# Attention pairs taken by twos, v loaded and weighed by pair, own x buffers for the first three batches

## The chip, the cores and the metric

The kernel runs on one core of a Trainium2 chip. The metric is device time in microseconds; the runs shown are whole executions without a profile, and one more execution was profiled. TensorE is called PE in the profile, VectorE DVE, ScalarE ACT, GpSimd POOL; SP is the engine whose queue issues most transfers.

## The reference

Two blocks follow each other. The first is a causal attention over 8 batches, 8 heads, 576 tokens and 64 numbers a head, whose scores get a bias from a running sum of `s`:

```
scores = q @ k.T / 8 + min(-(cum[i] - cum[j]), 0)     # cum = cumsum(max(s, 0)); later keys masked
x = softmax(scores) @ v                               # 8 batches x 576 tokens x 512
```

The second sends each token of `x` to one of 8 experts. The expert is the largest of 8 logits, unless a gate says that the token keeps the expert of the token before it; the output is the softmax weight of that expert times a two-layer network:

```
out[token] = p[e] * (relu(x @ w1[e]) @ w2[e])         # 512 -> 1024 -> 512
```

All numbers are float32.

## The kernel before

**Pairs.** The attention works on pairs of heads: 8 batches with 4 pairs each, 32 pairs in all (`NPAIR`). A pair's q and k lie in 128 partitions, one head in each half. Scores are computed with keys on the partitions. `scores(n, u)` does one of four units of pair n: matmuls (L869) into a PSUM buffer `ps` of which there are three, an exponential on ScalarE (L870) into a tile `e`, and the causal mask on GpSimd (L855). `values(n, j0, j1)` multiplies the `e` tiles with v (L894) for the token blocks 0 to 5 (PSUM tile `po0`) or 6 to 8 (`po6`), and its `evacuate` takes the reciprocal of the row sums (L900, kept in `recs`) and writes the scaled result into the batch's x tile `xb` (L901). `turn(n)` transposes the pair's part of x (L912) for the router's matmuls.

**Weighed v.** The bias is a product of two factors, so v is multiplied by a factor per key: `weigh` does this on VectorE (L841, for the first batch `weigh_heads`, L851) from the loaded tile `va` into the tiles `vg`, and `ones_column` copies the factor itself beside it on ScalarE (L833). v is loaded by batch, and there are two sets of `vg`, one for odd and one for even batches.

**Order.** The program order is written by hand and each engine keeps it. Slot n of the main loop issues the scores of pair n and then the values of pair n - 1:

```
for u in range(len(UNITS)):
    scores(n, u)
    if u == 1: at(n, 0)
values(n - 1, 0, NJA)()
at(n, 1)
values(n - 1, NJA, NJ)()
turn(n - 1)
at(n, 3)
```

Weighing and loads stand between these lines. `plan(slot, place, f)` notes work of the router, and `at(slot, place)` issues it there.

**Router.** The router works on groups of two batches (`GB`). For a group it runs `product` (matmuls into `lp`, L208) and `logits` (copies on VectorE, L217 to L226), `codes` (L233 to L245 on VectorE, with one exponential `ex` on ScalarE at L242), `turn1`, `turn2` (VectorE), `ranks` (matmuls into `pos`, L289 and L290, in one of the three buffers of the scores), `rows` and `gates` (VectorE), and then 18 scatters (`put`, L337 on GpSimd) that store the tokens of x in a table in the chip's main memory, sorted by expert. The fourth group's steps run in the experts' part.

**x tiles.** The pool `p_x` has four buffers; a small scratch for the key factors takes one, and the batches follow in turn.

**Experts.** `Experts.run` follows: units of up to 256 tokens, layer 1 (L568) and layer 2 (L592), with weights of one expert, 4 MB, loaded for each unit. The first unit's weights go into the pool `w_first` while the attention still runs; `fetch` reads its tokens from the table.

## Time and profile before

| | us |
|---|---|
| median of 3 runs (lowest, highest) | 740.49 (739.32, 741.26) |
| the profiled execution, its own time | 751.67 |
| its span, from the first to the last instruction | 749.9 |
| attention, up to the first expert matmul | 224.45 |
| TensorE busy in the span | 733.6 |
| ScalarE busy | 162.2 |
| VectorE busy | 246.8 |
| GpSimd busy | 209.4 |

A line of the groups names the line of the code, the engine, the operation, what is written from what, the shape and the count, then the busy time and the mean of one in ns, and after the second bar the time that the engine stood idle just before, with what ended it. A line of the timeline has the start in us, the duration in us, engine, line and operation, the count of merged instructions, and in brackets the idle time before it and what ended that. Matmul ends are modelled, so the starts are read. "issue" is time in which the engine waited for nothing that the profile shows.

### The profile page before, as it was taken

The page shows a single profiled execution, that of the slowest core. Times are in us where ns is not written, and L with a number is a line of the kernel's source. Part 1 is how long each engine was busy: PE and PEld are TensorE (multiplying, and loading weights), DVE is VectorE, ACT ScalarE, POOL GpSimd, SP SyncE. Part 2 cuts the span into 40 slices and gives each one's busy share as a digit, 9 for nine tenths or more (in the row PEclk, how much of TensorE's full clock was granted, in tenths as well). Part 3 has the DMA queues.
Part 4 walks back from the last instruction along what each step waited for, and adds up shares of the span by engine and source line. Part 5 has one row for each costly group of instructions (what it writes and reads, how often), then busy time and mean ns, then how long its engine had stood idle before and what let it go on. Part 6 is the DMA issues. An engine that isn't in the chain of part 4 may idle for free.

```text
span 749.9 us, 16025 instructions
## 1 busy us (share of the span) xinstructions
PE 733.6 (98%) x6509; PEld 501.5 (67%) x6509; DVE 246.8 (33%) x653; ACT 162.2 (22%) x318; POOL 209.4 (28%) x452
## 2 busy tenths in 40 slices
PE   8999999999999999999999999999999999999996
PEld 5888878877877667657657375537645676637674
DVE  4655756766765552101100511140142001050110
ACT  4554544443431011001001010101110111101110
POOL 2643376577575245330100101010101001000110
PEclk9999999999999999999999999999999999999999
DMA  6764464566679776698537969996999965999000
GB/s 205 249 198 130 146 203 140 189 197 200 214 224 369 243 301 212 257 409 227 219 131 224 377 195 397 365 393 241 423 324 370 413 215 227 297 394 339 30 15 32
DMA packets 55524, 186.23 MB, mean 248 GB/s; under 512 B 11661, under 2 KB 32525, under 8 KB 47120
## 3 DMA queue, kind: packets, MB, share of 16 engines
q1 hardware_dynamic: 48640, 165.01, 62.4%
q0 software_dynamic: 6800, 20.09, 7.1%
q8 instruction: 53, 0.87, 0.5%
q14 instruction: 31, 0.25, 0.1%
HBM read 164.46 MB, written 20.88 MB: 247 GB/s over the span
## 4 chain that ended last, share of the span: by engine, by line
PE 95%; issue 1%; DVE 1%; POOL 1%; ACT 0%; POOLq 0%; ACTq 0%
PE yp L592 34%; PE hp L568 31%; PE po L894 13%; PE ps L869 12%; PE hp L559 4%; PE lp L208 1%; POOL table L337 0%; ACT e L870 0%; PE pos L289 0%; POOL e L855 0%; PE pos L290 0%; DVE y L595 0%; POOL out_dram L597 0%; DVE xb L901 0%; POOLq L93 0%
## 5 line engine op out<-in xcount | busy, mean ns | idle before, releaser
L592 PE MATMUL yp<-w2b,hT 128*128 128x512 f32 (+2 forms) x752 | 259.3, 593 | 0.0
L568 PE MATMUL hp<-xT,w1b 128*128 128x256 f32 (+1 forms) x1216 | 233.2, 352 | 0.0
L568 PEld LDWEIGHTS hp<-xT,w1b 128*128 128x128 f32 x1216 | 206.2, 190 | 32.6 <-issue 7.5
L592 PEld LDWEIGHTS yp<-w2b,hT 128*128 128x128 f32 (+2 forms) x752 | 107.9, 167 | 141.0 <-issue 139.6
L597 POOL DMA_INDIRECT out_dram<-y,gi x37 | 36.5, 987 | 416.4 <-DVE y L595 391.5
L570 ACT ACTIVATE hT<-hp 128x256 f32<-128x256 f32 (+1 forms) x152 | 54.0, 355 | 430.7 <-PE hp L568 421.0
L595 DVE TENSOR_SCALAR y<-yp,gi 128x512 f32<-128x512 f32 x37 | 27.6, 746 | 304.6 <-PE yp L592 291.9
L870 ACT ACTIVATE e<-ps 128x768 f32<-128x768 f32 (+1 forms) x128 | 97.3, 837 | 104.3 <-PE ps L869 93.7
L894 PE MATMUL po<-vg,e 128*64 128x66 f32 x3200 | 106.7, 224 | 5.9 <-issue 3.6
L894 PEld LDWEIGHTS po<-vg,e 128*64 128x64 f32 x3200 | 99.2, 138 | 11.3 <-issue 7.2
L869 PE MATMUL ps<-qb,kb 64*128 64x192 f32 (+4 forms) x768 | 98.6, 402 | 0.8 <-ACT e L870 0.8
L869 PEld LDWEIGHTS ps<-qb,kb 64*128 64x128 f32 x768 | 67.3, 187 | 31.6 <-ACT e L870 9.5
L337 POOL DMA_INDIRECT table<-xb,idx x72 | 74.4, 1033 | 32.2 <-issue 23.0
L855 POOL TENSOR_SCALAR_AFFINE_SELECT e<-e 128x256 f32<-128x256 f32 (+1 forms) x160 | 64.0, 421 | 63.0 <-ACT e L870 62.2
L579 DVE STREAM_TRANSPOSE hT<-hs 32x256 f32<-32x256 f32 x64 | 27.9, 436 | 74.8 <-ACT hs L561 74.0
L900 DVE RECIPROCAL recs<-po 128x12 f32<-128x12 f32 x64 | 13.4, 209 | 63.1 <-PE po L894 55.7
L901 DVE TENSOR_TENSOR xb<-po,recs 128x384 f32<-128x384 f32 x64 | 29.3, 458 | 3.1 <-POOL xb L313 0.5
L841 DVE TENSOR_TENSOR vg<-va,wk 128x1024 f32<-128x1024 f32 (+1 forms) x21 | 29.4, 1400 | 2.2 <-DMA va<-in_vm_dram 2.2
L538 DVE STREAM_TRANSPOSE xT<-xq 128x1024 f32<-128x1024 f32 (+1 forms) x23 | 23.7, 1028 | 18.7 <-DMA xq<-table 18.5
L559 PE MATMUL hp<-w1b,xT 128*32 128x512 f32 (+1 forms) x224 | 28.3, 594 | 0.0
L912 DVE STREAM_TRANSPOSE xt<-xb 128x576 f32<-128x576 f32 x32 | 24.9, 778 | 2.9 <-PE lp L208 1.4
L559 PEld LDWEIGHTS hp<-w1b,xT 128*32 128x32 f32 (+1 forms) x224 | 8.1, 114 | 17.7 <-issue 17.6
(222 smaller groups left out, 165.7 us busy)
## 6 DMA issues: line engine op xcount, KB each, us to landing
w1b<-in_w_dram SPq DMA_DIRECT2D x29, 2048.0 KB
w2b<-in_w_dram SPq DMA_DIRECT2D x29, 2048.0 KB
kb<-in_k_dram SPq DMA_DIRECT2D x32, 288.0 KB
qb<-in_q_dram SPq DMA_DIRECT2D x32, 288.0 KB
xq<-table SPq DMA_DIRECT2D x56, 130.0 KB
va<-in_vm_dram SPq DMA_DIRECT2D x7, 1024.0 KB
w1b<-in_w_dram SPq DMA_DIRECT2D x4, 512.0 KB
w2b<-in_w_dram SPq DMA_DIRECT2D x4, 512.0 KB
```

Of the source, the lines that this page charges most:

```text
L337: put = self.nc.gpsimd.indirect_dma_start(out=self.halves, in_=src, element_offset=0, in_offset=None, out_offset=bass.IndirectOffsetOnAxis ...
L559: mm(ps[d, :], lhsT=xT[:, k, d], rhs=self.ws[l][0][:, k, c * 512 : c * 512 + 512], start=(k == 0), stop=(k == DK - 1))
L568: mm(ps[:, :w], lhsT=self.ws[ls[0]][0][:, k, c * P : c * P + P], rhs=xT[:, k, :w], start=(k == 0), stop=(k == DK - 1))
L570: nc.scalar.activation(self.hT[u][:, c, :w], ps[:, :w], Act.Relu)
L592: mm(ps[d, :], lhsT=hT[:, k, n * P + d.start : n * P + d.stop], rhs=self.ws[l][1][:, k, :], start=(k == 0), stop=(k == FK - 1))
L597: put = nc.gpsimd.indirect_dma_start(out=self.out[:, :], out_offset=bass.IndirectOffsetOnAxis(ap=gi.bitcast(I32)[:, n, 0:1], axis=0), in_= ...
L841: nc.vector.tensor_tensor(vgs[b % 2][g][:, c0:c1].rearrange("p c h e -> p (c h) e")[:, :, :DH], va[:, c0:c1].rearrange("p c h e -> p (c h) ...
L855: nc.gpsimd.affine_select(out=ap, in_=ap, compare_op=Alu.is_ge, fill=0.0, base=base, pattern=n, channel_multiplier=-1)
L869: mm(ps[:, h, at : at + z - a], lhsT=kb[d, key : key + P], rhs=qb[d, a:z], start=True, stop=True)
L870: nc.scalar.activation(e, ps, Act.Exp, scale=scale)
L894: mm(po[d, j - j0, :], lhsT=weights_of(n, c, j, h), rhs=vg[:, c, 2 * hp + h, :], start=(c == 0), stop=(c == last))
L901: nc.vector.tensor_tensor(xb[:, j0:j1, :, 32 * hp : 32 * hp + 32], po[:, :, :DH].rearrange("p j (g i) -> p j g i", g=2), rec[:, :, 0].unsq ...
```

## The change

The loop now runs over 16 slots m of two pairs, 2m and 2m + 1. A slot issues the scores of both pairs, then the values of both, then both turns, then the weighing for the two pairs that come two slots later. v comes from the host already laid out by pair, with zeros for the missing tokens of the last block; a pair is one load of 320 KB into one of four `va` buffers, and is weighed by two VectorE operations and one ScalarE copy into one of four `vg` tiles. The x tiles of batches 0 and 1 lie in the space of the first expert's weights (`w_first`), that of batch 2 in a tile of its own, and only the later ones in `p_x`. The router's steps move to places of the new slots: 0 and 1 after the scores of the first and second pair, 3 and 4 after their values, 5 at the end of the slot. Its constants are set in two parts.

```diff
-PARTS = ((0, 1), (1, HP))
+NV = 4
+STORES = (((4, 5), (0, 1, 3, 4, 5), (0, 1, 3, 4, 5), (0, 1, 3, 4, 5), (0,)), ((4, 5, 5), (0, 1, 3, 4, 5), (0, 1, 3, 4, 5), (0, 1, 3, 4, 5)),
+          ((4, 5), (0, 0, 1, 1, 3, 4, 5, 5)))
+BX = 3
...
-    def load_v(b):
-        if b >= B:
+    def load_v(n):
+        if n >= NPAIR:
             return
-        nc.sync.dma_start(va[:, :NF], vm[b])
-        nc.sync.dma_start(va[TL:, NF], vt[b])
+        b, hp = divmod(n, HP)
+        va = vs[n] = p_v.tile([P, NB, 2, DH], F32, name="va")
+        nc.sync.dma_start(va.rearrange("p c h d -> p (c h d)"), v[b, hp].rearrange("p c h d -> p (c h d)"))
...
+    def weigh(n):
+        if n >= NPAIR:
             return
+        va, vg = vs.pop(n), vgs[n % NV]
+        nc.scalar.copy(vg[:, :, :, VW - 2 : VW - 1].rearrange("p c h e -> p (c h) e"),
+                       wk[:, n].rearrange("p c h -> p (c h)").unsqueeze(2))
+        for to, c in ((slice(0, G1), G1), (slice(G1, G1 + NB), NB)):
+            nc.vector.tensor_tensor(vg[:, to].rearrange("p c h e -> p (c h) e")[:, :, :DH],
+                                    va[:, :c].rearrange("p c h e -> p (c h) e"),
+                                    wk[:, n, to].rearrange("p c h -> p (c h)").unsqueeze(2).to_broadcast([P, c * 2, DH]),
+                                    op=Alu.mult)
...
+    def x_tile(b):
+        if b == 2:
+            return p_x0.tile([P, NJ, 2, XW], F32, name="xb0")
+        w = experts.w_first.tile([P, FK, D] if b else [P, DK, F], F32, name=f"w{b + 1}b")
+        return w.rearrange("p c f -> p (c f)")[:, : NJ * 2 * XW].rearrange("p (j g f) -> p j g f", j=NJ, g=2)
...
     for g in range(NG - 1):
+        m = HP * GB // 2 * (g + 1)
+        plan(m, 1, lambda g=g: router.product(g, of(g), banks))
+        plan(m, 3, lambda g=g: router.logits(g))
+        plan(m, 5, lambda g=g: (router.codes(g), router.turn1(g)))
+        plan(m + 1, 3, lambda g=g: router.turn2(g))
+        plan(m + 1, 5, lambda g=g: router.gates(g, [xs[b] for b in range(g * GB, g * GB + GB)]))
+        plan(m + 2, 1, lambda g=g: router.ranks(g, banks))
+        plan(m + 2, 3, lambda g=g: router.rows(g))
+        places = [(m + 2 + i, p) for i, ps in enumerate(STORES[g]) for p in ps]
...
+    m = NPAIR // 2
+    plan(1, 5, router.constants)
+    plan(2, 5, router.constants2)
+    plan(2, 3, range_ends)
+    plan(m - 5, 5, lambda: router.assign_early(0))
     for i in range(4):
+        plan(m - 4 + i // 2, (1, 5)[i % 2], lambda i=i: experts.load(0, None, i))
+    plan(m - 2, 0, lambda: (experts.fetch(0), experts.fetch(1)))
...
+    for m in range(NPAIR // 2):
+        pair = 2 * m, 2 * m + 1
+        for n in pair:
+            if m:
+                load_v(n + NV + 2)
+            for u in range(len(UNITS)):
+                if (n, u) == (0, 3):
+                    key_exps()
                 scores(n, u)
+                if (n, u) == (1, 0):
+                    key_weights()
+                    weigh(0)
+                    weigh(1)
+            load_qk(n + NV)
+            at(m, n - 2 * m)
+        for n in pair:
+            values(n, 0, NJA)()
+            values(n, NJA, NJ)()
+            at(m, 3 + n - 2 * m)
+        for n in pair:
+            turn(n)
+        for n in range(2 * m + (NV if m else 2), 2 * m + NV + 2):
+            if not m:
+                load_v(n + 2)
+            weigh(n)
+        at(m, 5)
```

More of the change, by code (lines that the diff above doesn't have):

```diff
@@ L64 @@
     k: bass.AP,
-    vm: bass.AP,
-    vt: bass.AP,
+    v: bass.AP,
     s: bass.AP,
@@ L89 @@
         with ExitStack() as early:
-            attention(early, tc, q, k, vm, vt, s, wx, ident, recs, wend, router, experts)
+            attention(early, tc, q, k, v, s, wx, ident, recs, wend, router, experts)
         experts.run(recs, wend, out_of)
@@ L104 @@
             gate = g.tile([P, NBLK], F32, name="gate")
-            attention_general(tc, q, k, vm, vt, s, w_gate, w_local, cum_d, x_d, ident, lg)
+            attention_general(tc, q, k, v, s, w_gate, w_local, cum_d, x_d, ident, lg)
             route(tc, ident, lg, ebi, idx_g, idx_s, gate)
@@ L119, in constants @@
     def constants(self):
-        nc, ident, table = self.nc, self.ident, self.table
+        nc = self.nc
         self.ones = self.t("r_ones", [P, P])
@@ L127, in constants @@
         self.eidx = self.lane[:, :E]
+        self.base0 = self.t("base0", [P, E])
+        nc.gpsimd.tensor_scalar(self.base0, self.eidx, float(CAP), 0.0, Alu.mult, Alu.add)
+        self.base = self.t("base", [P, E])
+        nc.gpsimd.tensor_copy(self.base, self.base0)
         self.low = self.t("low", [P, E])
@@ L143, in constants, with constants2 @@
         nc.gpsimd.tensor_scalar(self.cbase[DH:], self.cbase[DH:], 1.0, -float(E * DH), Alu.mult, Alu.add)
+    def constants2(self):
+        nc, table = self.nc, self.table
         self.thr = self.t("thr", [P, NC])
@@ L162, in constants @@
                                     channel_multiplier=-1)
-        self.base0 = self.t("base0", [P, E])
-        nc.gpsimd.tensor_scalar(self.base0, self.eidx, float(CAP), 0.0, Alu.mult, Alu.add)
-        self.base = self.t("base", [P, E])
-        nc.gpsimd.tensor_copy(self.base, self.base0)
         self.cd = self.t("cd", [P, 32])
@@ L720, in run, with attention @@
         assert not todo and not self.puts
-def attention(ctx, tc, q, k, vm, vt, s, wx, ident, recs, wend, router, experts):
+def attention(ctx, tc, q, k, v, s, wx, ident, recs, wend, router, experts):
     nc = tc.nc
@@ L732, in attention @@
     p_in = pool("p_in", 4)
+    p_v = pool("p_v", NV)
     p_e = pool("p_e", 2)
     p_x = experts.p_x
+    p_x0 = pool("p_x0", 1)
     p_xt = pool("p_xt0", 1)
@@ L740, in banks @@
         return ps_s.tile([P, 2, 512], F32, name=name, tag="s")
-    ins, es, xs, xts = {}, {}, {}, {}
+    ins, vs, es, xs, xts = {}, {}, {}, {}, {}
     heads = [slice(DH * h, DH * h + DH) for h in range(2)]
@@ L767, in attention @@
     nc.vector.memset(ones, 1.0)
-    va = once.tile([P, NB, H, DH], F32, name="va")
-    vgs = [[once.tile([P, c, H, VW], F32, name=f"vg{g}{i}") for g, c in enumerate((G1, NB))] for i in range(2)]
+    vgs = [once.tile([P, G1 + NB, 2, VW], F32, name=f"vg{i}") for i in range(NV)]
     load_qk(1)
-    for a0, a1 in PARTS:
-        hs = slice(2 * a0, 2 * a1)
-        nc.sync.dma_start(va[:, :NF, hs], vm[0][:, :, hs])
-        nc.sync.dma_start(va[TL:, NF, hs], vt[0][:, hs])
-    for n in range(2, 4):
-        load_qk(n)
-    router.projection(wx)
-    wk1 = once.tile([P, B, G1, H], F32, name="wk1")
-    wk2 = once.tile([P, B, NB, H], F32, name="wk2")
-    for t in (va[:TL, NF], wk2[:TL, :, NF]):
-        nc.gpsimd.memset(t, 0.0)
-    for t in (*vgs[0], *vgs[1]):
+    load_v(0)
+    load_v(1)
+    load_qk(2)
+    load_v(2)
+    load_qk(3)
+    load_v(3)
+    router.projection(wx)
+    wk = once.tile([P, NPAIR, G1 + NB, 2], F32, name="wk")
+    nc.gpsimd.memset(wk[:TL, :, G1 + NF], 0.0)
+    for t in vgs:
         nc.gpsimd.memset(t[..., VW - 1 : VW], 1.0)
-    for t in vgs:
-        nc.gpsimd.memset(t[1][:TL, NF, :, VW - 1 : VW], 0.0)
+        nc.gpsimd.memset(t[:TL, G1 + NF, :, VW - 1 : VW], 0.0)
     def warm_up(n):
@@ L812, in key_weights @@
                 i += 1
-        i = 0
-        for wk, n in ((wk1, G1), (wk2, NB)):
-            for c in range(n):
-                d = slice(TL if c == NF else 0, P)
-                nc.vector.tensor_copy(wk[d, :, c, :].rearrange("p b (a h) -> p h b a", h=2),
-                                      cps[d, i].rearrange("p (h b a) -> p h b a", h=2, b=B))
-                i += 1
+        for i in range(G1 + NB):
+            d = slice(TL if i == G1 + NF else 0, P)
+            nc.vector.tensor_copy(wk[d, :, i, :].rearrange("p n h -> p h n"), cps[d, i].rearrange("p (h n) -> p h n", h=2))
     def range_ends():
@@ L829, in range_ends @@
             nc.sync.dma_start(wend[d], ends_d[h : h + 1].to_broadcast([DH, NPAIR * NJ]))
-    def ones_column(b, g, c0, c1):
-        to = vgs[b % 2][g][:, c0:c1].rearrange("p c h e -> p (c h) e")
-        nc.scalar.copy(to[:, :, VW - 2 : VW - 1],
-                       (wk1, wk2)[g][:, b, c0:c1].rearrange("p c h -> p (c h)").unsqueeze(2))
-    def weigh(b, g, c0, c1):
-        if b >= B:
-            return
-        w = (wk1, wk2)[g][:, b, c0:c1].rearrange("p c h -> p (c h)").unsqueeze(2)
-        nc.vector.tensor_tensor(vgs[b % 2][g][:, c0:c1].rearrange("p c h e -> p (c h) e")[:, :, :DH],
-                                va[:, c0:c1].rearrange("p c h e -> p (c h) e"),
-                                w.to_broadcast([P, (c1 - c0) * H, DH]), op=Alu.mult)
-        ones_column(b, g, c0, c1)
-    def weigh_heads(a0, a1):
-        hs = slice(2 * a0, 2 * a1)
-        for g, c in enumerate((G1, NB)):
-            to = vgs[0][g][:, :, hs, :DH]
-            nc.vector.tensor_tensor(to, va[:, :c, hs], (wk1, wk2)[g][:, 0, :, hs].unsqueeze(3)
-                                    .to_broadcast(list(to.shape)), op=Alu.mult)
+    def weigh(n):
+        if n >= NPAIR:
+            return
+        va, vg = vs.pop(n), vgs[n % NV]
[6 more added lines that the diff above has]
+                                    op=Alu.mult)
     def masked(ap, n, base=0):
@@ L880, in weights_of @@
                     return es[n][u][:, h, at + j * DH - a : at + j * DH - a + DH]
+    def x_tile(b):
[3 more added lines that the diff above has]
+        return w.rearrange("p c f -> p (c f)")[:, : NJ * 2 * XW].rearrange("p (j g f) -> p j g f", j=NJ, g=2)
     def values(n, j0, j1):
         b, hp = divmod(n, HP)
-        g, bl = divmod(b, GB)
         if b not in xs:
-            xs[b] = p_x.tile([P, NJ, 2, XW], F32, name="xb")
+            xs[b] = x_tile(b) if b < BX else p_x.tile([P, NJ, 2, XW], F32, name="xb")
         xb = xs[b]
@@ L892, in values @@
                 for h, d in enumerate(heads):
-                    vg = vgs[b % 2][0 if j < 2 * G1 else 1]
-                    mm(po[d, j - j0, :], lhsT=weights_of(n, c, j, h), rhs=vg[:, c, 2 * hp + h, :],
+                    mm(po[d, j - j0, :], lhsT=weights_of(n, c, j, h),
+                       rhs=vgs[n % NV][:, c if j < 2 * G1 else G1 + c, h, :],
                        start=(c == 0), stop=(c == last))
@@ L922, in attention @@
     for g in range(NG - 1):
-        n = HP * GB * (g + 1)
-        plan(n + 1, 3, lambda g=g: router.product(g, of(g), banks))
-        plan(n + 1, 3, lambda g=g: router.logits(g))
-        plan(n + 2, 1, lambda g=g: router.codes(g))
-        plan(n + 3, 1, lambda g=g: router.turn1(g))
-        plan(n + 3, 3, lambda g=g: router.turn2(g))
-        plan(n + 4, 3, lambda g=g: router.ranks(g, banks))
-        plan(n + 4, 3, lambda g=g: router.rows(g))
-        plan(n + 5, 1, lambda g=g: router.gates(g, [xs[b] for b in range(g * GB, g * GB + GB)]))
-        places = []
-        for m in range(n + 5, n + 13):
-            if m - n in (6, 7, 8) and m < NPAIR:
-                places.append((m, 0))
-            places += [(m, 1), (m, 3)] if m <= NPAIR else []
+        m = HP * GB // 2 * (g + 1)
[7 more added lines that the diff above has]
+        places = [(m + 2 + i, p) for i, ps in enumerate(STORES[g]) for p in ps]
         for c in range(NC):
@@ L940, in attention @@
                 continue
-            m, p = places[c]
-            after = recs[0:1, m - 1, 0 if p < 3 else NJA, 0:1] if p else None
-            plan(m, p, lambda g=g, c=c, after=after: router.scatter(g, c, after))
-    plan(3, 3, router.constants)
-    n = NPAIR - HP + 1
-    plan(n, 3, lambda: router.product(NG - 1, (xts[B - 2],), banks, (0,)))
-    plan(n, 3, lambda: router.logits(NG - 1, (0,)))
-    plan(5, 3, range_ends)
-    n = 2 * HP * GB
-    plan(n + 7, 1, lambda: router.assign_early(0))
-    for i in range(4):
-        plan(n + 9 + i, 3, lambda i=i: experts.load(0, None, i))
-    plan(n + 13, 1, lambda: (experts.fetch(0), experts.fetch(1)))
-    plan(n + 14, 1, lambda: router.assign_early(1))
-    plan(n + 15, 3, lambda: experts.turn_x(0))
+            i, p = places[c]
+            after = {3: (2 * i, NJA), 4: (2 * i + 1, 0), 5: (2 * i + 1, NJA)}.get(p)
+            after = after and recs[0:1, after[0], after[1], 0:1]
+            plan(i, p, lambda g=g, c=c, after=after: router.scatter(g, c, after))
+    m = NPAIR // 2
[3 more added lines that the diff above has]
+    plan(m - 5, 5, lambda: router.assign_early(0))
+    for i in range(4):
+        plan(m - 4 + i // 2, (1, 5)[i % 2], lambda i=i: experts.load(0, None, i))
+    plan(m - 2, 0, lambda: (experts.fetch(0), experts.fetch(1)))
+    plan(m - 2, 4, lambda: router.product(NG - 1, (xts[B - 2],), banks, (0,)))
+    plan(m - 2, 4, lambda: router.logits(NG - 1, (0,)))
+    plan(m - 1, 0, lambda: experts.turn_x(0))
+    plan(m - 1, 0, lambda: router.assign_early(1))
     def at(slot, place):
@@ L959, in at @@
             f()
-    for n in range(NPAIR + 1):
-        b, hp = divmod(n, HP)
-        if n == 0:
-            for u in range(3):
-                scores(0, u)
-            key_exps()
-            scores(0, 3)
-            scores(1, 0)
-            key_weights()
-            ones_column(0, 0, 0, G1)
-            ones_column(0, 1, 0, NB)
-            weigh_heads(*PARTS[0])
-            scores(1, 1)
-            continue
-        if n > 1:
-            load_qk(n + 4)
-        for u in range(len(UNITS)):
-            if n > 1:
-                scores(n, u)
-            if u == 1:
-                at(n, 0)
-        values(n - 1, 0, NJA)()
-        at(n, 1)
-        if n == 1:
-            scores(1, 2)
-            scores(1, 3)
-            weigh_heads(1, 2)
-        if b:
-            if hp == 1:
-                weigh(b + 1, 1, 0, 3)
-            if hp == 2:
-                weigh(b + 1, 1, 3, NB)
-                load_v(b + 2)
-        elif hp == 3:
-            weigh(1, 1, 0, 3)
-        values(n - 1, NJA, NJ)()
-        turn(n - 1)
-        if hp == 0:
-            weigh(b + 1, 0, 0, G1)
-        if n == 1:
-            weigh_heads(2, HP)
-            load_v(1)
-            load_qk(4)
-            load_qk(5)
-        if n == 2:
-            weigh(1, 0, 0, G1)
-        if n == 3:
-            weigh(1, 1, 3, NB)
-            load_v(2)
-        at(n, 3)
+    for m in range(NPAIR // 2):
[6 more added lines that the diff above has]
+                    key_exps()
+                scores(n, u)
+                if (n, u) == (1, 0):
[15 more added lines that the diff above has]
+        at(m, 5)
     assert not todo
@@ L1046, in attention_general @@
 @with_exitstack
-def attention_general(ctx, tc, q, k, vm, vt, s, w_gate, w_local, cum_d, x_d, ident, lg):
+def attention_general(ctx, tc, q, k, v, s, w_gate, w_local, cum_d, x_d, ident, lg):
     nc = tc.nc
@@ L1080, in load_batch @@
         nc.sync.dma_start(kb, k[b])
-        nc.sync.dma_start(vb, vm[b])
-        nc.sync.dma_start(vl, vt[b])
+        for hp in range(HP):
+            hs = slice(2 * hp, 2 * hp + 2)
+            nc.sync.dma_start(vb[:, :, hs], v[b, hp][:, :NF])
+            nc.sync.dma_start(vl[:, hs], v[b, hp][TL:, NF])
         ins[b] = qb, kb, vb, vl
@@ L1554, in heads @@
         return a.reshape(B, HP, 2, S, DH).transpose(0, 2, 4, 1, 3).reshape(B, P, HP, S)
-    v = i["v"]
+    v = _np.zeros((B, HP, P, NB, 2, DH), _np.float32)
+    of = i["v"].reshape(B, HP, 2, S, DH)
+    v[:, :, :, :NF] = of[:, :, :, :TS].reshape(B, HP, 2, NF, P, DH).transpose(0, 1, 4, 3, 2, 5)
+    v[:, :, TL:, NF] = of[:, :, :, TS:].transpose(0, 1, 3, 2, 4)
     wx = _np.zeros((2, 2, 32, HP, 2, 2, WR), _np.float32)
@@ L1563 @@
         "k": heads(i["k"]),
-        "vm": v[:, :, :TS].reshape(B, H, NF, P, DH).transpose(0, 3, 2, 1, 4),
-        "vt": v[:, :, TS:].transpose(0, 2, 1, 3),
+        "v": v,
         "s": i["s"].reshape(B * H, S),
```

## The prediction

> **What bounds the kernel now.** I read the head of the page first, then its groups, then the timeline of the attention part, then the waits. TensorE is busy 98% of the span, and the attention (up to 224.45, where the experts' L568 starts) is a strict alternation of score matmuls (L869) and value matmuls (L894):

> ```profile
> span 749.9 us, 16025 instructions
> PE 733.6 (98%) x6509; PEld 501.5 (67%) x6509; DVE 246.8 (33%) x653; ACT 162.2 (22%) x318; POOL 209.4 (28%) x452
> L870 ACT ACTIVATE e<-ps 128x768 f32<-128x768 f32 (+1 forms) x128 | 97.3, 837 | 104.3 <-PE ps L869 93.7
> L894 PE MATMUL po<-vg,e 128*64 128x66 f32 x3200 | 106.7, 224 | 5.9 <-issue 3.6
> L869 PE MATMUL ps<-qb,kb 64*128 64x192 f32 (+4 forms) x768 | 98.6, 402 | 0.8 <-ACT e L870 0.8
> ```

> The timeline of TensorE shows the rhythm, one undisturbed pair being 75.15 - 69.13 = 6.02 us: 2.96 from the first score matmul to the first value matmul, 3.06 back.

> ```profile
> 69.13 3.02 PE L869 MATMUL ps<-qb,kb 64*128 64x384 f32 x24
> 72.09 3.14 PE L894 MATMUL po<-vg,e 128*64 128x66 f32 x100
> 75.15 3.02 PE L869 MATMUL ps<-qb,kb 64*128 64x384 f32 x24
> ```

> Each stage changes the shape of the array (64*128, 128*64), and TensorE sets the pace; ScalarE waits for it (93.7 us), not the reverse. The third thing to see is the one router step in which ScalarE waits for VectorE. This is the merged timeline of the slot in which `codes` runs today:

> ```profile
> 73.75 0.23 DVE L900 RECIPROCAL recs<-po 128x12 f32<-128x12 f32 x1 [1.52 <-PE po L894]
> 74.02 0.56 DVE L901 TENSOR_TENSOR xb<-po,recs 128x384 f32<-128x384 f32 x1
> 74.50 0.29 DVE L233 TENSOR_REDUCE mx<-l 128x18 f32<-128x144 f32 x1
> ...
> 75.59 0.32 ACT L242 ACTIVATE ex<-ex 128x144 f32<-128x144 f32 x1 [2.41 <-DVE top L239]
> ...
> 76.18 0.81 ACT L870 ACTIVATE e<-ps 128x768 f32<-128x768 f32 x1 [0.16 <-PE ps L869]
> ```

> The router's exponential waits for VectorE until 75.59, and the next score exponential is still on time at 76.18, because `codes` runs ahead of nearly everything else that VectorE has to do in that slot.

> [...] The trace shows the slow clock only at the start: the four warm-up matmuls of 512 columns last 3.78 us together, where sixteen of that width take 6.87 us in the experts. [...]

> **The change part by part.** The sum is made against the profiled execution: 751.67 us, its span of 749.9 and 1.8 around it. That is 11.2 above the median of 740.49. I put the 11 us down to stalls marked "issue" inside value and router stages (103.86 to 108.74 is 4.88 where 3.06 is normal; 158.44 to 163.29 is 4.85; 172.62 to 177.20 is 4.58; smaller ones make up some 9.5 in the value stages). They would then belong to profiling and I carry the differences over to the median unchanged.

> *Fewer changes of shape.* Steady values: between 72.31 and 74.5 the timeline starts 76 matmuls, 28.8 ns each, so 100 take 2.9 us. [...] 32 value stages become 16, so 16 x 0.4 = **-6.4 us**, on the path. Bounds: 4 and 7.

> *Start.* The first values wait at 12.67 for the weighed v (weight load idle 0.94). The changed order has the last two score units of pair 1 to put there: **-0.8**. Bounds 0 and -1.

> *Router's rank matmuls.* They now precede value matmuls, not scores. Before, they held one of the three score buffers: twice a score stage takes 3.54 (87.91 to 91.45) where 2.96 is normal: **-1.2**. At the end, TensorE idles 0.53 for a mask (220.18): **-0.5**.

> *Loads and weighing by pair.* A pair of v is 128 x 640 numbers, 320 KB, instead of 1,152 KB a batch; four buffers put each load about one slot of 12 us ahead of its use, and the transfers stay hidden behind the matmuls as before. VectorE's weighing has the same 896 elements per partition and pair (about 1.05 us, from 1.22 for 1024 elements). The queue of SP gets longer by waits for `weigh` before a load of v, with loads of q and k behind it; these have a slot in hand. Own x buffers: the scatters of batches 0 and 1 end in slot 10, the weights that take the same space load from slot 12. All 0; if v came late, the next weighing and then the values of two slots on would wait.

> *ScalarE with eight units in a row.* A score unit takes about 0.69 us of TensorE, an exponential about 0.73 (four lie in the 2.9 to 3.0 us of a stage), the first one starts 1.03 after the stage (69.13 to 70.16). With three score buffers the sixth to eighth unit come within 0.1 to 0.2 us of waiting for one. Taken as **0**, bounds 0 and 0.25 a slot, 4 in all.

> *`codes` at the end of a slot.* This decides. It moves to place 5 of slots 4, 8 and 12: behind both turns and both weighings on VectorE, and on ScalarE ahead of all eight exponentials of the next slot. The order of ScalarE's instructions in the changed program says so: two copies of the weight column, `ex`, then the eight. Count from the first value matmul of the slot's first pair (0). Both value stages end at E = 5.8 + 0.15 = 6.0.
> - First pair's two evacuations end at 3.65 (last matmul 2.9, then 0.23 and 0.36 and gaps).
> - `logits` (place 3): 69.94 to 72.24 before, 2.3, to 5.95.
> - Second pair's evacuations, now all ready: 0.75 + 0.6, to 7.3.
> - Two turns of 0.78: 8.9. Two weighings: 2.1, to 11.0.
> - `codes` up to `ex`: 74.50 to 75.59 before, 1.09, to 12.1. `ex` and hand-over 0.25: 12.4.

> The next score exponential would have started at E + 1.03 = 7.05; it is 5.3 late. TensorE fills the three score buffers and stops at E + 2.15 until about 13.35: **5.2 us idle, three times, +15.6**. After it ScalarE and TensorE run level, so nothing is won back. Bounds: without the delay by `logits`, 4.5; with VectorE slowed by GpSimd or v, 6.5. Then the clock: [...] Estimate 0.8 each, **+2.4**, bounds 0 and 7.

> *The rest.* `turn2`, `rows` and `gates` also lie between evacuations, but no exponential waits for them; masks on GpSimd finish ahead of their values by over 0.5 us even with five scatters a slot (1.2 each in 12 us). The experts start from the same state, and their weights have slack: unit 1's weights are issued by 226.6 and used at 255.8.

> Sum: -6.4 - 0.8 - 1.2 - 0.5 + 15.6 + 2.4 = **+9.1**. Profiled 751.67 becomes about 761, the median 740.49 about 749.6; I take **749.5**.

> **The rivals.**
> - *Drains win (faster).* The three waits are short: if `ex` were ready by 3 us after E instead of 6, three score buffers would cover most of it and -8.9 would stand: 740.5 - 8.9 = 731.6. The turning point is 8.9 / 3 = 3.0 us of idle per wait. For it: before, `ex` never held TensorE. Against it: two turns and two weighings alone are 3.7 after E + 0.6.
> - *ScalarE bound.* The eight units also cost 0.25 each slot: +4, 753.5. For it: 2.92 against 2.75 per four units; against it: the lead of three buffers.
> - *Drains are worth nothing.* [...] the change does not save what it says: 749.5 + 6.4 = 756. [...]
> - *Issue stalls are real.* If they are in unprofiled runs too and smaller v loads remove half of them, -5: 744.5.

> **How the numbers follow.** The forecast with its bounds (745 to 754) has 0.65; ScalarE bound or a heavier clock loss 0.12; no gain by drains 0.04; issue stalls removed 0.07, half of it within 0.3% (2.2 us, about what can be told from no change); drains win 0.12, a little of it within. Faster 0.11, same 0.06, slower 0.83. The range 742 to 757 leaves out most of the faster cases and the end of the heavier ones, 0.18 together.

> **What would show it.** Right: three stretches without matmuls of about 5 us, at the start of slots 5, 9 and 13 (near 70, 125 and 180), the fourth score unit waiting for ScalarE, ScalarE for `top` of VectorE, and possibly a dip in the granted clock; elsewhere a slot of two pairs of about 11.6 us instead of 12.04. Wrong: no such stretches (then the chain on VectorE is mis-sized), or slots still of 12 us or more (then drains or ScalarE's rate are).

## The result and the profile after

| | before | after |
|---|---|---|
| median, us (lowest, highest) | 740.61 (739.32, 741.26) | 759.91 (757.59, 761.01) |
| profiled execution, its own time | 739.21 (profiled again beside the first experiments) | 759.36 |
| its span | 737.5 | 757.5 |
| attention, up to the first expert matmul | 213.73 | 233.71 |

The ratio is 1.0259, 95% interval 1.023 to 1.0287: slower by 19.3 us, where 9 had been forecast. The predicted time, 749.5, had a range up to 757. Before was profiled a second time, because the profile above belongs to an execution that was itself 11 us slow; all comparisons below use the second one. The attention ends 20.0 us later (233.71 - 213.73), and this is the whole difference.

The page of after, head and groups, columns as before:

```profile
span 757.5 us, 16110 instructions
PE 730.7 (96%) x6509; PEld 500.4 (66%) x6509; DVE 257.1 (34%) x690; ACT 165.2 (22%) x327; POOL 209.9 (28%) x453
L859 PE MATMUL ps<-qb,kb 64*128 64x192 f32 (+4 forms) x768 | 102.2, 420 | 13.4 <-ACT e L860 12.8
L889 PE MATMUL po<-vg,e 128*64 128x66 f32 x3200 | 99.1, 223 | 4.4 <-issue 2.7
L860 ACT ACTIVATE e<-ps 128x768 f32<-128x768 f32 (+1 forms) x128 | 96.6, 847 | 24.6 <-PE ps L859 22.7
```

The scores (L859) now stand idle 13.4 us, nearly all of it for the exponentials; it was 0.8. ScalarE no longer waits only for TensorE. Four of the waits between 14 and 234 us (engine, tile and line, what is waited for; total, times, longest) say who made ScalarE late, and what else TensorE waited for:

```profile
ACT ex L247 <- DVE top L244: 15.4, 3, 5.3
PE ps L859 <- ACT e L860: 12.6, 3, 4.4
PE po L889 <- issue: 2.7, 5, 0.7
PE po L889 <- DVE recs L896: 1.7, 2, 1.4
```

Three times, and only three, the router's exponential `ex` waits for VectorE and TensorE for the exponential behind it. The other two lines are small, but the prediction's sum had neither. Each of the four is read below.

**The slots without router work.** The timeline of TensorE in after:

```profile
26.32 6.05 PE L889 MATMUL po<-vg,e 128*64 128x66 f32 x200
32.31 5.83 PE L859 MATMUL ps<-qb,kb 64*128 64x384 f32 x48
38.07 5.23 PE L889 MATMUL po<-vg,e 128*64 128x66 f32 x171
43.78 0.39 PE L889 MATMUL po<-vg,e 128*64 128x66 f32 x6 [0.48 <-issue]
```

Values to scores is 32.31 - 26.32 = 5.99, scores to values 38.07 - 32.31 = 5.76: 11.75 a slot, where two pairs of before are 12.04. One change of shape there and back is worth 0.30 us, 4.8 in 16 slots. The last line is a stall in the middle of a value stage, between matmuls that wait for nothing that the trace shows: the start before it is at 43.08, so it lasts 43.78 - 43.08 = 0.70, where 0.03 is normal.

**The slots of `codes`.** Slot 5, from the timelines of VectorE, ScalarE and TensorE in after:

```profile
72.55 0.20 DVE L896 RECIPROCAL recs<-po 128x6 f32<-128x6 f32 x1 [0.22 <-PE po L889]
...
73.05 1.43 DVE L908 STREAM_TRANSPOSE xt<-xb 128x576 f32<-128x576 f32 x2
74.41 2.19 DVE L839 TENSOR_TENSOR vg<-va,wk 128x256 f32<-128x256 f32 x4
76.51 0.29 DVE L238 TENSOR_REDUCE mx<-l 128x18 f32<-128x144 f32 x1
...
77.26 0.31 DVE L244 SCALAR_TENSOR_TENSOR top<-ex,low 128x144 f32<-128x144 f32 x1
...
77.60 0.32 ACT L247 ACTIVATE ex<-ex 128x144 f32<-128x144 f32 x1 [4.84 <-DVE top L244]
77.83 1.49 ACT L860 ACTIVATE e<-ps 128x768 f32<-128x768 f32 x2
...
73.68 1.08 PE L859 MATMUL ps<-qb,kb 64*128 64x192 f32 x6
78.67 5.47 PE L859 MATMUL ps<-qb,kb 64*128 64x320 f32 x32 [3.92 <-ACT e L860]
```

Evacuation, two turns, four weighing operations, then `codes`: `ex` starts at 77.60, which is 12.0 after the stage's first value matmul (65.58); the prediction's chain said 12.1. TensorE fills its score buffers and stands still; the gap between the starts of two matmuls is 78.67 - 74.22 = 4.45 (4.93 and 4.84 in slots 9 and 13). Then it runs slowly. The granted clock is the column after the five engines' busy times in these windows of after:

```profile
78.67:81.00 2.33, 2.33 (x14) 1.58 (x16) 1.02 (x5) 2.16 (x3) 1.36 (x4) 0.67 0.15 20
81.00:83.00 2.00, 2.00 (x14) 1.60 (x12) 0.00 (x0) 1.34 (x2) 0.96 (x3) 0.53 0.92 322
83.00:86.00 3.00, 3.00 (x77) 2.59 (x75) 0.23 (x1) 1.91 (x3) 1.58 (x6) 1.00 0.45 133
```

It falls to about half (0.53 from 81 to 83) and is back at 83 (1.00). The score stages of slots 5, 9 and 13 take 11.63, 12.11 and 12.64 in place of 5.76: 5.87, 6.35 and 6.88 more, **19.1 us** together.

**The last slot.** Its second value stage (timeline of TensorE) waits for the evacuation of `po0`, because `turn_x` (L543) and `assign_early(1)` (L359 to L415) stand ahead of it on VectorE from 224.09 to 229.77:

```profile
226.11 3.14 PE L889 MATMUL po<-vg,e 128*64 128x66 f32 x100
230.65 3.14 PE L889 MATMUL po<-vg,e 128*64 128x66 f32 x100 [1.40 <-DVE recs L896]
```

That is 1.62 from matmul to matmul (229.03 to 230.65).

**The stalls.** Eight gaps of 0.17 to 0.96 us in after, seven of them in value stages, 5.0 us in all, have one thing in common. Number TensorE's instructions in order, two for each matmul of the trace (weight load and matmul) and one for each further instruction that its sequencer records: all eight lie at number 192 or 193 of a group of 256. (A matmul of the program stands in the trace as two.) Each ends 1.25 to 1.57 us after the end of a transfer of 16,384 bytes on the queue that the page calls "instruction". There are 53 such transfers in the trace of after and 13,143 recorded instructions of TensorE, 248 to a transfer. That TensorE waits there for its instructions ("fetch" in the expectations) is my reading; the trace shows the place and the transfer. I call places with this number "marks"; most of them are crossed without a stall. The value stage of after is one run of 200 matmuls, 400 instructions in 6 us, so that two marks, 3.7 us apart, can lie inside it; a value stage of before has 200 instructions and can hold only one. Stalls at marks are rarer there, but they occur: two of the issue stalls in the first profile of before, 0.42 us (at 34.28) and 0.35 us (at 40.76), lie at a mark too, 1.4 us after such a transfer.

The difference, put together from the traces of after and the second profile of before: 19.1 (slots 5, 9, 13) + 5.0 (marks) + 2.1 (values that wait for VectorE, 1.62 and 0.51) + 1.0 (start, below) - 4.5 (shape, slots 1 to 15) - 1.2 (ranks) - 1.8 (two stalls that before has) = 19.7, of 20.0.

### The profile page after: what moved, and what is told of

Read it like the earlier page. It is cut to its first block, busy times and chain, and to the rows that moved or that the text cites. A ratio compares the mean times of both kernels' runs of the same rounds, so it can differ in the third digit from the quotient of the medians.

```text
span 757.5 us, 16110 instructions
## 1 busy us (share of the span) xinstructions
PE 730.7 (96%) x6509; PEld 500.4 (66%) x6509; DVE 257.1 (34%) x690; ACT 165.2 (22%) x327; POOL 209.9 (28%) x453
## 4 chain that ended last, share of the span: by engine, by line
PE 91%; DVE 6%; issue 1%; DMA 1%; ACT 1%; SPq 0%; POOL 0%; POOLq 0%; ACTq 0%; DVEq 0%
PE yp L597 34%; PE hp L573 30%; PE po L889 11%; PE ps L859 10%; PE hp L564 4%; DVE vg L839 1%; PE lp L213 1%; DVE xt L908 1%; DVE xb L897 1%; DVE l L228 1%; DMA xb<-in_s_dram 1%; ACT e L860 0%; DVE recs L896 0%; DVE xb L799 0%; PE pos L294 0%
## 5 line engine op out<-in xcount | busy, mean ns | idle before, releaser
L859 PE MATMUL ps<-qb,kb 64*128 64x192 f32 (+4 forms) x768 | 102.2, 420 | 13.4 <-ACT e L860 12.8
L889 PE MATMUL po<-vg,e 128*64 128x66 f32 x3200 | 99.1, 223 | 4.4 <-issue 2.7
L889 PEld LDWEIGHTS po<-vg,e 128*64 128x64 f32 x3200 | 95.9, 138 | 7.3 <-issue 4.3
L859 PEld LDWEIGHTS ps<-qb,kb 64*128 64x128 f32 x768 | 69.7, 199 | 45.3 <-ACT e L860 27.4
L845 POOL TENSOR_SCALAR_AFFINE_SELECT e<-e 128x256 f32<-128x256 f32 (+1 forms) x160 | 71.6, 472 | 69.5 <-ACT e L860 68.8
L342 POOL DMA_INDIRECT table<-xb,idx x54 | 53.6, 992 | 17.5 <-issue 14.8
L839 DVE TENSOR_TENSOR vg<-va,wk 128x256 f32<-128x256 f32 x64 | 44.4, 755 | 0.0
L543 DVE STREAM_TRANSPOSE xT<-xq 128x1024 f32<-128x1024 f32 (+1 forms) x23 | 23.7, 1029 | 16.1 <-DMA xq<-table 15.8
L836 ACT COPY vg<-wk 128x14 f32<-128x14 f32 x32 | 6.7, 216 | 79.8 <-PE po L889 79.3
L897 DVE TENSOR_TENSOR xb<-po,recs 128x384 f32<-128x384 f32 (+1 forms) x48 | 22.0, 457 | 1.9 <-POOL e L845 0.2
## 6 DMA issues: line engine op xcount, KB each, us to landing
w1b<-in_w_dram SPq DMA_DIRECT2D x29, 2048.0 KB, 10.3
```

The source lines that it names most:

```text
L342: put = self.nc.gpsimd.indirect_dma_start(out=self.halves, in_=src, element_offset=0, in_offset=None, out_offset=bass.IndirectOffsetOnAxis ...
L839: nc.vector.tensor_tensor(vg[:, to].rearrange("p c h e -> p (c h) e")[:, :, :DH], va[:, :c].rearrange("p c h e -> p (c h) e"), wk[:, n, to ...
L845: nc.gpsimd.affine_select(out=ap, in_=ap, compare_op=Alu.is_ge, fill=0.0, base=base, pattern=n, channel_multiplier=-1)
L859: mm(ps[:, h, at : at + z - a], lhsT=kb[d, key : key + P], rhs=qb[d, a:z], start=True, stop=True)
L889: mm(po[d, j - j0, :], lhsT=weights_of(n, c, j, h), rhs=vgs[n % NV][:, c if j < 2 * G1 else G1 + c, h, :], start=(c == 0), stop=(c == last))
L897: nc.vector.tensor_tensor(xb[:, j0:j1, :, 32 * hp : 32 * hp + 32], po[:, :, :DH].rearrange("p j (g i) -> p j g i", g=2), rec[:, :, 0].unsq ...
```

## The experiments

My theory: VectorE's order makes ScalarE late three times, with a clock loss behind it (19 us); the rest is the stalls at marks. The rivals are with each experiment.

**Before again.** The unchanged kernel, one execution.

> The kernel before, unchanged, looked at once more. Two readings of the first profile compete. A: the stalls marked issue in its value stages (about 9.5 us) belong to that one execution and are not in the timed runs; then this profiled execution is near 741 us, its attention ends near 215 instead of 224.45, and a slot of two pairs takes 12.04. B: they are part of every execution; then the profile again shows about 750 with the same stalls.

739.21; the executions of before that were timed beside the experiments have a median of 741.27 (34 of them, for the first two ratios below) and of 740.99 (28, for the later ones). An undisturbed slot of two pairs is 12.04 throughout, and only two value stages lose more than 0.12 us (0.53 at 161.17; 1.31 at 211.01, which the trace puts down to a mask on GpSimd; the place is a mark as well, but no instruction transfer ended in the 5.6 us before it). The many issue stalls in value stages of the first profile belong to that execution. The line of the values on the page has 2.1 us of idle time in place of 5.9, and the largest part of it is that mask, not "issue":

```profile
L894 PE MATMUL po<-vg,e 128*64 128x66 f32 x3200 | 101.0, 223 | 2.1 <-POOL e L855 1.1
```

**The exponential moved off the path.** Only `ex` moves: from `codes` to the beginning of `turn2`, one slot later.

```diff
 def codes(self, g):
-        self.nc.scalar.activation(ex, ex, Act.Exp)
...
 def turn2(self, g):
+        self.nc.scalar.activation(st["ex"], st["ex"], Act.Exp)
```

> The changed kernel with only the router's exponential on ScalarE moved, from the end of slots 4, 8 and 12 to the place of turn2 in slots 5, 9 and 13, behind the eight score exponentials; VectorE's order is the same. Theory A (ScalarE's queue was held by that one instruction): the three idle stretches of 4.5 to 4.9 us and the slow scores after them go, the slots 5, 9 and 13 lose 5.9, 6.4 and 6.9 us, 19 in all, and the time is about 741. Rival (VectorE itself is behind, and the values of the next slot would wait for it anyway): the idle time moves to the value stages and less than 8 us are gained, 752 or more.

744.06 (741.93 to 747.13), ratio to before 1.0038 [1.0025, 1.0051]. The score stages of slots 5, 9 and 13 are 5.76 again and the clock stays full (1.00 over the first 213 us): some 16 us of the 19.3 went with one instruction. Part of the lateness comes back where VectorE now matters alone, and the marks stall 7.9 us in the values of this execution. Timeline of TensorE, slot 5:

```profile
72.39 5.83 PE L859 MATMUL ps<-qb,kb 64*128 64x384 f32 x48
78.15 3.14 PE L889 MATMUL po<-vg,e 128*64 128x66 f32 x100
81.75 0.92 PE L889 MATMUL po<-vg,e 128*64 128x66 f32 x24 [0.47 <-DVE recs L896]
83.44 2.44 PE L889 MATMUL po<-vg,e 128*64 128x66 f32 x76 [0.77 <-issue]
```

The second line runs without a wait and the third starts 0.69 late for the evacuation of the first pair; slots 9 and 13 have 1.51 and 1.41 there. The fourth is a mark.

**`codes` first.** The other way to the same end: `codes` at place 4, ahead of turns and weighings.

```diff
-        plan(m, 5, lambda g=g: (router.codes(g), router.turn1(g)))
+        plan(m, 4, lambda g=g: router.codes(g))
+        plan(m, 5, lambda g=g: router.turn1(g))
```

> The changed kernel with codes issued ahead of the two turns and the two weighings of slots 4, 8 and 12 (turn1 stays at the end of the slot). VectorE then has 1.4 + 2.1 = 3.5 us less before the router's exponential. If the idle time of TensorE follows the chain on VectorE one for one, the three stretches of 4.5 to 4.9 us shrink to about 1.0 to 1.4[...], and the time is about 745 (three times 5.0 less). If the clock loss or another wait holds the time, it stays above 750.

745.31 (741.89 to 748.25), ratio 1.0051 [1.0036, 1.0066]. The waits shrink to gaps of 1.20, 1.68 and 1.68 and the score stages to 6.85, 7.33 and 7.34; the clock stays full (mean 0.999 over the profiled execution, 0.987 in after). So it is the place of `codes` behind turns and weighings that counts, and these waits of under 1.7 us cost no clock. Timeline of TensorE, slot 5:

```profile
72.51 2.32 PE L859 MATMUL ps<-qb,kb 64*128 64x384 f32 x16
75.49 3.94 PE L859 MATMUL ps<-qb,kb 64*128 64x320 f32 x32 [0.66 <-ACT e L860]
```

**The numbering shifted.** After with one of the two warm-up matmuls and 33 tiny ones at the start, 128 instructions more.

```diff
-    warm_up(2)
+    warm_up(1)
+    tick = banks("tick")[:, 0]
+    for i in range(33):
+        mm(tick[:32, :16], lhsT=zero[:, :32], rhs=zero[:, :16], start=True, stop=True)
```

> The changed kernel with one of its two warm-up matmuls replaced by 33 tiny ones, so that TensorE's stream is 128 instructions longer from the start. Theory F (the stalls marked issue in the value stages are late fetches of instructions: all six stand at instruction 192 or 193 of a group of 256, and end about 1.3 us after a transfer of the instruction queue): the stalls move by half a group. In the trace of the changed kernel, half-shifted groups fall wholly inside value stages from slot 4 on and not before; so slots 2 and 3 (38 to 58 us) lose their stalls, and new ones, if any, stand in other places at instruction 192 or 193 of the longer stream. Rival (they come from bulk transfers at those moments): slots 2, 3 and 4 stall as before, near the same matmuls of their value stages.

764.06, one execution; the tiny matmuls delayed the start by 2.3 us (first scores at 7.16 in place of 4.84), so the time says little. The trace does: the value stages of slots 2 and 3, which stall in every other run of this order that was profiled before, now take 5.98 us, and the stalls sit in slots 4 to 14, up to 1.89 us each, again all at 192 or 193. Where a slot stalls in both traces, it does so 1.9 us further into its values (slot 6: 5.54 us after their start, in after 3.67), and 128 instructions of a value stage take 1.9 us. The stalls move with the numbering and not with the work.

**VectorE's work spread.** `ex` later as above, `turn1` one place later beside `turn2`, `assign_early(1)` behind the last values.

```diff
-        plan(m, 5, lambda g=g: (router.codes(g), router.turn1(g)))
-        plan(m + 1, 3, lambda g=g: router.turn2(g))
+        plan(m, 5, lambda g=g: router.codes(g))
+        plan(m + 1, 3, lambda g=g: (router.turn1(g), router.turn2(g)))
...
-    plan(m - 1, 0, lambda: router.assign_early(1))
+    plan(m - 1, 5, lambda: router.assign_early(1))
```

> After with three moves: the exponential `ex` at the start of turn2 (as in e1_ex_later), codes alone at the end of slots 4, 8 and 12 with turn1 one place later beside turn2, and assign_early(1) from the first place of slot 15 to its end. Theory (ScalarE's and VectorE's order make the waits, instruction fetch makes the rest): the three waits for late evacuations in the values of slots 5, 9 and 13 (0.69, 1.51 and 1.41 us in e1_ex_later) and the 1.6 us at the end of the attention shrink to about 0, so about 739 to 740, level with before; the stalls at instruction 192 or 193 of 256 stay, 5 to 8 us in all. Rival (VectorE is simply short of time in these slots): the waits turn up elsewhere and the time stays near 744.

741.09 (739.06 to 745.74), ratio to before 1.0006 [0.9991, 1.0021]: the same time as before. The three waits and the one at the end are gone; one of 1.05 us stays, in slot 10, where `gates` delays an evacuation. `gates` is not alone in this: the third weighing operation of slot 9, just ahead of it, lasts 2.0 us in this trace and in after, beside five masks on GpSimd, where the same one of slot 5 lasts 0.6 and that of slot 4 in after, with no mask beside it, 0.42. The marks stall 7.2 us in the values: slot 5 has the mark and nothing else.

```profile
76.99 3.84 PE L889 MATMUL po<-vg,e 128*64 128x66 f32 x124
81.39 2.44 PE L889 MATMUL po<-vg,e 128*64 128x66 f32 x76 [0.57 <-issue]
```

**Loads at the start of the slot.** The same kernel, with the 1.8 MB of a slot issued before its scores.

```diff
-            if m:
-                load_v(n + NV + 2)
+            if m > 1 and n == 2 * m:
+                for i in pair:
+                    load_qk(i + 2)
+                for i in pair:
+                    load_v(i + NV)
...
-            load_qk(n + NV)
+            if m == 0:
+                load_qk(n + NV)
```

> e4_spread with the loads of slots 2 to 15 issued at the start of the slot (q and k of the next two pairs, v of the two after), so that the 1.8 MB that used to land during the values now land mostly during the scores. Theory (a fetch of instructions is late when bulk transfers are under way[...]): the stalls at index 192 or 193 fall from 5 to 8 us to 2 or less, so about 734 to 736, below before. Rival (the length of the values' run alone decides[...]): the stalls stay and the time is that of e4_spread within 1 us.

741.08 (738.34 to 744.86), ratio to before 0.9998 [0.9984, 1.0013]. The stalls at marks became fewer but longer: five in the values, 7.6 us in all, where the kernel without the early loads has ten; the longest is 2.90 us (timeline of TensorE, slot 3):

```profile
49.55 5.35 PE L889 MATMUL po<-vg,e 128*64 128x66 f32 x176
57.59 0.92 PE L889 MATMUL po<-vg,e 128*64 128x66 f32 x24 [2.68 <-issue]
```

The expected gain is not there. When the bulk transfers are issued does not decide what the stalls cost in sum; what makes one mark stall and the next not stays open. The longest stall shows this much: the transfer itself takes 1.0 us (55.36 to 56.37), about as long as others of its kind, but it starts only when TensorE already stands, since 54.69.

**One change of shape more.** In 15 slots, one matmul of the scores' form between the values of the two pairs.

```diff
             at(m, 3 + n - 2 * m)
+            if n == 2 * m and n + 2 < NPAIR:
+                qb, kb = ins[n + 2]
+                mm(banks("tick")[:, 0, :DH], lhsT=kb[heads[0], :P], rhs=qb[heads[0], :DH], start=True, stop=True)
```

> e4_spread with one matmul of the scores' form (128 x 64 result, its result unused) between the values of the first and the second pair in 15 slots: one more change to the scores' form and back. Theory (there and back costs 0.30 us, as 0.30 us a slot went away in after): from the last value matmul of the first pair to the first of the second 0.30 us more than in e4_spread, and the matmul's own 0.05 to 0.1 us; 15 times 0.35 to 0.4 is 5 to 6 us. Rival (0.40 as the prediction had it): 7 us or more. Rival (a change of form costs nothing and the 0.30 us is from elsewhere): 1 to 1.5 us.

743.93 (743.27 to 746.23), 2.8 above the kernel that it extends, where 5 to 6 had been expected. Its timeline of TensorE in slot 7:

```profile
104.08 3.14 PE L889 MATMUL po<-vg,e 128*64 128x66 f32 x100
107.15 0.43 PE L974 MATMUL tick<-qb,kb 64*128 64x64 f32 x2
107.51 2.67 PE L889 MATMUL po<-vg,e 128*64 128x66 f32 x84
```

The two halves take 3.07 + 0.36 + 3.07 = 6.50 in place of 5.98: 0.52 more. Two such matmuls at full clock are an estimated 0.23 of it (36 take 4.09 us in a later experiment), dearer than the 0.05 to 0.1 expected. That leaves 0.29 for the change itself, as expected. But 15 x 0.52 is 7.8 and the time rose by 2.8: the cut value stages stall 4.2 us at their marks in place of 7.2, and the wait for VectorE and one stall in the scores, 1.8 us together in the trace of the kernel that it extends, are not there.

**The marks held in place.** Small matmuls ahead of the scores of some slots, so that the values begin at a chosen distance behind a mark; they precede the first score unit. The second kernel leaves out the entry for slot 1.

```diff
+PADS = {1: 44, 4: 41, 8: 41, 12: 41, 15: 38}
...
+        if m in PADS:
+            qb, kb = ins[2 * m]
+            tick = banks("tick")
+            for i in range(PADS[m]):
+                mm(tick[:, 0, :16], lhsT=kb[heads[0], :P], rhs=qb[heads[0], :16], start=True, stop=True)
```

> e4_spread with small matmuls of the scores' form (128 x 16, results unused) ahead of the scores of slots 1, 4, 8, 12 and 15 (44, 41, 41, 41, 38 of them, four TensorE instructions each), so that the values of each slot from 1 on begin 65 to 105 instructions behind the mark (index 193 of 256 in our count): one mark then lies in the first 2.8 us of the values and the next one behind them. Their own time, some 15 to 25 us, is not the question. Theory [...]: the stalls of instruction fetch in the values of slots 1 to 15 fall from 6.1 us in nine places to 2 us or less. Rival (a fetch is late for reasons of the transfers alone): 5 to 8 us of stalls as in e4_spread.

> The same with small matmuls ahead of slots 4, 8, 12 and 15 only (41, 41, 41, 38), so that the values of each slot begin 150 to 185 instructions behind the mark: a mark in the first 1.6 us and a second one 4.7 to 5.9 us into the values. Their own time is 10 to 20 us. Theory: stalls in the values of nearly all the slots, at the second mark, 8 to 14 us in all. Rival (transfers alone): 5 to 8 us as in e4_spread, in any of the slots.

817.37 and 805.23, one execution each; the small matmuls were dearer than expected, in part because the clock fell under them (0.50 from 27.67 to 34.93 in the first). What was asked: with the marks early, no value stage of slots 1 to 15 has a stall at a mark; two score stages right behind the values have one, and are 1.3 and 0.7 us longer. With two marks in each, nine of fifteen value stages have one, 0.12 to 2.08 us, 9.5 us in all, and no score stage. First the kernel with early marks, slot 1, then the other, slot 7 (timelines of TensorE):

```profile
43.32 6.05 PE L890 MATMUL po<-vg,e 128*64 128x66 f32 x200
49.31 5.83 PE L860 MATMUL ps<-qb,kb 64*128 64x384 f32 x48
```

```profile
117.14 5.35 PE L890 MATMUL po<-vg,e 128*64 128x66 f32 x176
124.34 0.92 PE L890 MATMUL po<-vg,e 128*64 128x66 f32 x24 [1.85 <-issue]
```

So the cause is shown: where the run of instructions lies against the marks (0 us of stalls in these stages, and 9.5), not the transfers alone. The run need not be of values only: in after and the kernel with VectorE's work spread, the values of slot 8, right behind the router's 64 product matmuls, stall at a mark that comes already 2.2 us in (0.17 and 0.73 us).

**The idle time filled, thin.** After with 18 matmuls of 64 rows and 64 columns (36 in the trace) where TensorE waits in slots 5, 9 and 13, written into a free value buffer.

```diff
+                if (n, u) in ((10, 3), (18, 3), (26, 3)):
+                    qb, kb = ins[n]
+                    tick = ps_o.tile([P, NJ - NJA, VW], F32, name=f"po{NJA}")
+                    for i in range(18):
+                        mm(tick[:, 0, :DH], lhsT=kb[heads[0], :P], rhs=qb[heads[0], :DH], start=True, stop=True)
                 scores(n, u)
```

> After with 18 matmuls of the scores' form (128 x 64, results unused) ahead of the fourth score unit in slots 5, 9 and 13, where TensorE stands idle 4.45 to 4.93 us for ScalarE; they take some 3 to 4 us of that idle time. Theory (the idle time costs 4.45 to 4.93 us and the half clock after it another 1.4 to 2.0 us a slot): the clock stays full, and the score stages of these slots shrink from 11.63, 12.11 and 12.64 us to 10.2 to 10.6 us, some 5 us in all. Rival (the half-speed scores are limited by ScalarE's late exponentials, not by the clock): the stages stay within 0.3 us of what they were.

765.93, one execution. TensorE is busy without a break in slot 5, and the clock falls all the same; the score stage takes 11.64 us (11.63 in after). Its windows in slot 5, the filling first and then the scores after it:

```profile
75.52:79.61 4.09, 4.09 (x39) 3.99 (x36) 3.83 (x13) 1.07 (x3) 0.00 (x0) 1.00 0.29 84
79.61:85.01 5.40, 5.40 (x34) 3.87 (x33) 1.01 (x5) 4.31 (x6) 2.74 (x7) 0.68 0.51 170
```

In slot 13 a stall of 2.36 us at a mark came first and the filling itself then ran at half speed (clock 0.50 from 193.04): 35 of its matmuls last 7.56 us, where 36 last 4.12 in slot 5.

**The idle time filled, dense.** The same with 10 matmuls (20 in the trace) of all 128 rows and 192 columns.

```diff
-                    for i in range(18):
-                        mm(tick[:, 0, :DH], lhsT=kb[heads[0], :P], rhs=qb[heads[0], :DH], start=True, stop=True)
+                    tick = tick.rearrange("p j e -> p (j e)")[:, : 3 * DH]
+                    for i in range(10):
+                        mm(tick, lhsT=kb[:, :P], rhs=qb[:, : 3 * DH], start=True, stop=True)
```

> After with 10 dense matmuls (all 128 rows, 128 x 192, results unused) ahead of the fourth score unit in slots 5, 9 and 13, in place of the 18 thin ones (64 rows, 128 x 64) of e9_keep_busy, which filled the idle time and did not keep the clock; they take some 3.2 to 3.5 us. Theory [...]: the granted clock stays at 1.00 over the score stages of these slots, and they take 10 to 10.6 us in place of 11.6 to 12.6, some 4 to 5 us less in all. Rival (the clock falls for another reason than the idle time, or ScalarE's late exponentials set the pace of the scores after it): clock 0.5 to 0.8 there and 11.3 us or more each, as in e9_keep_busy.

754.06, one execution. The clock stays full (1.00 in the windows of all three slots) and the score stages of slots 5, 9 and 13 take 10.11, 10.02 and 10.03 us: 1.5, 2.1 and 2.6 less than in after, 6.2 in all. Windows of slot 5, and the line of TensorE's timeline behind the wait:

```profile
73.44:77.43 3.99, 3.52 (x23) 3.22 (x21) 3.73 (x13) 1.08 (x3) 0.00 (x0) 1.00 0.28 82
77.43:81.29 3.86, 3.86 (x32) 2.57 (x32) 1.01 (x5) 3.86 (x6) 2.56 (x7) 1.00 0.44 97
```

```profile
77.43 3.94 PE L859 MATMUL ps<-qb,kb 64*128 64x320 f32 x32 [0.47 <-ACT e L860]
```

The 32 matmuls behind the wait take 3.87 us at the full clock, in the three slots here and with `codes` first. In after they take 5.40, 5.40 and 6.02: 1.53, 1.53 and 2.15 more. This splits the 19.1 us: 5.2 is the clock, the other 13.9 the wait for `ex`. The last 1.0 of the 6.2 is not the clock: in slots 9 and 13 the wait itself is half a microsecond shorter here (4.38 us from matmul to matmul), behind values that stalls at marks held up by 1.01 and 1.29 us.

No version beat both kernels: the best two, with VectorE's work spread, are level with before.

## Why the prediction was right or wrong

- **The deciding step, `codes` at the end of a slot: right in mechanism and nearly in size.** Three waits in the predicted slots, behind the predicted work, the fourth score unit waiting. Predicted 15.6 of idle and 2.4 of clock, 18.0 in all; measured 13.9 and 5.2, together 19.1. That the total came so near is in part luck, because one term was 1.7 too large and the other 2.8 too small. The idle term: TensorE went on 12.7 to 13.1 us after the first value matmul (12.9 in slot 9, 136.62 - 123.72), not 13.35, and in slot 5 the values ended 0.8 later by a mark, with a wait 0.4 to 0.5 shorter than in slots 9 and 13. The clock term was less than half of what came. Its 0.8 a slot was an estimate of mine that no trace of before gives. The clock fell in all three slots (0.50 from 79.47, 137.50 and 192.11), and in the filled slots 5 and 9 of the thin filling too (0.68 in the scores of slot 5; in slot 9, 24 score matmuls last 5.92 us, where 32 last 3.94 at the full clock). Gaps of 4.45 us or more lost the clock, and gaps for `ex` of up to 1.68 us did not (mean 0.999). But the length of the gap does not decide alone, and the runs do not give the rule: a stall of 2.90 us kept the clock (1.00 over the first 100 us, loads at the start of the slot), one of 2.36 us lost it (0.50, thin filling, slot 13), and in the first slot of after it fell at 11.21 (to 0.50), though TensorE had been busy for 2.39 of the 3.41 us before.
- **Fewer changes of shape: right in sign, mis-sized.** The 0.4 us for one change there and back was an estimate of mine; the traces give 0.30 by the slot and 0.29 by the added change: -4.8 in place of -6.4. "Drains", my word for this cost, is not shown: the traces have the time of a change and not what TensorE does in it.
- **Start.** In the dense-filling run the values of slot 0 end at 18.76, where before has done the same work at 19.56 (22.51 less one score stage of 2.95): the predicted -0.8. In after's profile they end at 20.56, because the scores between 11.21 and 14.62 ran at half the clock (0.50), for which the prediction had no term; with VectorE's work spread a mark took it. So it was +1.0 in the profiled execution.
- **Ranks: right**, 1.2 in the second profile of before too. **The mask at the end**: its wait of 0.53 is 1.31 in that profile; after has none there.
- **"The rest" at nothing: wrong.** `turn2` and `rows` delayed nothing, but `gates`, at the end of slot 9 behind the slow weighing, made an evacuation of slot 10 0.51 late, and `turn_x` with `assign_early(1)`, ahead of the last pairs' evacuations, 1.62. I asked only whether an exponential waits. The values wait for evacuations too, as each pair writes the same `po0`.
- **Missing altogether: 5.0 us of stalls at marks.** I had read "issue" stalls as belonging to the one profiled execution, and for nearly all of before's that was right. The conclusion that the change doesn't touch them was the step that failed: it doubled the unbroken run of short instructions, from 200 to 400, past the 256 from one mark to the next. The rival "issue stalls are real" had the sign wrong: they were nearly absent before and came with the change.
- **ScalarE with eight units in a row**: 0 was right; undisturbed score stages of 48 matmuls take 5.76 with no wait.
- **Loads and weighing by pair**: 0; no value waits for v in the trace.

The miss of 10.4 us (759.9 - 749.5) is then: marks 5.0, VectorE 2.1, start 1.8, shape 1.6, the waits 1.1, less what before's own two stalls gave back beyond the 0.5 taken for the mask (1.3): 10.3.

## What to carry to other kernels

When work is regrouped, write each engine's new order down and ask of every step what stands behind it on its own queue, evacuations as well as exponentials; here the place of one activation of 0.32 us was worth 16 us. What fewer changes of shape save can be lost again to the longer runs: 4.8 us were saved here, and 5 to 8 us of stalls at marks came. Count the instructions of a run of short matmuls: here runs of 400 stalled at marks, 5.0 us in after, and runs of 200 seldom did (0.42 and 0.35 us in the first profile of before).
